# Sigmoid attention and MLP on one core: one wait ahead of each attention group, and a fourth of the attention's rate during the half-size up products

## The chip, the core and the metric

The kernel runs on one core of a Trainium2 chip. The metric is the device time of one execution in microseconds (us): median of 3 runs, 1158.67 us before the change (1157.67 to 1159.39). A profile of one execution goes with it. Engines are named as in the profile: PE is the matrix engine (TensorE), PEld its weight loads, DVE VectorE, ACT ScalarE, POOL GpSimd, SP the engine that issues most DMAs.

## The reference

Sigmoid attention over 8 batches, 12 heads, 448 positions and head size 64, in float32, followed by a two-layer MLP with a piecewise quadratic between the layers (768 to 2048 to 768 wide, 3584 tokens):

```python
scores = scale * np.matmul(q, k.transpose(0, 1, 3, 2)) - np.log(S)
attn = 1.0 / (1.0 + np.exp(-scores))
x = np.matmul(attn, v)            # then (B, H, S, D) -> (B*S, H*D)
h = x @ w_in
g = np.where(h >= 1, h, np.where(h <= -1, 0.0, (h + 1) ** 2 / 4))
out = g @ w_out
```

## The kernel before

**Attention.** Two heads make a pair; a batch has 6 pairs, the whole run 48. The 448 keys of a pair are cut into 4 pieces: c = 0, 1 and 2 with 128 keys each, and the "mid" piece c = 3 with the last 64 keys of both heads stacked. `load_pair` fetches q, k and v, `prep_a` finds maxima (on ACT), `prep_b` splits each float32 operand into two float16 halves (on POOL from pair 17 on) and sends them by DMA into the layout `qk`. `scores` makes the products of queries and keys into a PSUM tile `psc` (two buffers, so piece i reuses the buffer of piece i - 2), `weigh` applies the sigmoid in place (ACT, L450), and splits the result into a high half (ACT, L458) and a low half (DVE, L459) in `ahl`. `av` multiplies these with v into `pav`. From pair 14 on (`NFULL + NHALF`) `step` works on two pieces at once: `scores` of a group of two pieces, then `av` of the group before it. At a pair's last piece `av` ends with a copy into `x32` (ACT, L500) and a maximum `xm` (DVE, L501).

PE works on three kinds of product here. Full-array products take all 128 rows and columns: up (`ph`, L685 and L719), down (`po`, L755), the first part of the scores (L409 with `qk`, L404 for the mid piece), the column sums and maxima with `one` (L155, L171). The score corrections L418 take 64 rows, and the products with v L491 put out 64 columns; two of these that follow each other with different halves run side by side.

**MLP.** The attention of batch b + 1 is done while the MLP of batch b runs. For batch 2 and later (`SB`) the up projection is done in half-size products: 16 blocks of hidden units are treated as 8 pairs, each with 7 units of 9 matmuls over 224 columns (`up_blocks`), 56 units in all. They are followed by 48 down units (`downs`), each of 6 matmuls over 448 columns, 288 in all. `bend`, the activation between the layers, works on ACT and DVE during the up units.

**The order.** The loop at the end of the function (L894 to L930) emits units one by one, and between them steps of the attention, at a rate given by `share`: each of the first 92 units (`last`) counts `DW` = 8 in batches 2 to 7, so 56/92 of a batch's 24 pieces are emitted during the up units and the rest during the first 36 down units. At unit 92 `start_blocks` and `finish_blocks` are emitted: they take the maximum over the batch's x (`xm1`, L523), put it on a diagonal (`diag`, L161), spread it with a matmul (L171), reduce it (L172), make scales of it (L127 to L135), and split sums and differences of x (L534 to L537, on DVE and POOL) into the operands of the next batch's up products (L540 on ACT, L541 on DVE, seven of each). Which instruction stands where on each engine is settled at build time, by a scheduler that takes what is emitted first by preference but passes over what it holds not to be ready. On the chip each engine then goes through its instructions in that fixed order.

Of the kernel before, what the change touches and what calls it, by code (L numbers as in the profile page):

```python
# [14 lines left out]
F32 = mybir.dt.float32  # L15
# [8 lines left out]
P = 128  # L24
# [29 lines left out]
QA = 17  # L54
QT = 3
CORN = 10
TP = 1

DW = 8
MIX0 = 24  # L60
MIX1 = 96
Q_PRIO = 72
# [7 lines left out]
def sigmoid_attention_mlp(ctx: ExitStack, tc: tile.TileContext, first_qvk, qkv, w_in, w_out, out_t):  # L70
# [312 lines left out]

    pieces = {}

    def scores(todo):

        tiles = []
        for i in todo:
            p, c = divmod(i, NPC)  # L390
            mid = c == NKC
            w = slice(c * P, S if mid else (c + 1) * P)
            psc = ps_sc.tile([P, 2, 512], F32, tag="psc", name="psc")
            tiles.append(psc)
            if p < NFULL:
                r = ready[p][0]
                for j in range(2):
                    out = psc[j * D : (j + 1) * D, 0, :S] if mid else psc[:, j, :S]
                    rows = slice(j * D, (j + 1) * D)
                    nc.tensor.matmul(out, r[rows, 2, w], r[rows, 0, :], start=True, stop=True)  # L400
            elif mid and p >= NFULL + NHALF:
                hl = ready[p][4]
                for t, (kh, qh) in enumerate(((0, 0), (1, 0), (0, 1))):
                    nc.tensor.matmul(psc[:, 0, :S], corner(p)[:, kh, :], hl[:, 0, qh, :], start=t == 0, stop=t == 2)  # L404
            else:
                kq = ready[p][0]
                for j in range(2):
                    out = psc[j * D : (j + 1) * D, 0, :S] if mid else psc[:, j, :S]
                    nc.tensor.matmul(out, kq[:, j, 1, w], kq[:, j, 0, :], start=True, stop=False)  # L409
        for i, psc in zip(todo, tiles):  # L410
            p, c = divmod(i, NPC)
            mid = c == NKC
            if p >= NFULL and not (mid and p >= NFULL + NHALF):
                hl, w = ready[p][4], slice(c * P, S if mid else (c + 1) * P)
                for j in range(2):
                    rows = slice(j * D, (j + 1) * D)
                    out = psc[rows, 0, :S] if mid else psc[:, j, :S]
                    nc.tensor.matmul(out, hl[rows, 1, 0, w], hl[rows, 0, 1, :], start=False, stop=True)  # L418
            if mid and p >= NFULL + NHALF and p + 2 in maxes:

                sums[p + 2] = all_sum(maxes[p + 2], 3, psc[:, 1, :])
        for i, psc in zip(todo, tiles):
            weigh(i, psc)
        for p, c in (divmod(i, NPC) for i in todo):
# [13 lines left out]
    def weigh(i, psc):  # L438
# [5 lines left out]
        sqk = 1.0 / math.sqrt(D) if p < NFULL else ready[p][2][:, 0:1]  # L444
        if p < NFULL + NHALF:
            a32 = att_p.tile([P, 2, S], F32, tag="ahl", name="a32")
            nc.scalar.activation(a32[:, :n, :], a, AF.Sigmoid, bias=nls, scale=sqk)  # L447
            pieces[i] = a32
            return
        nc.scalar.activation(a, a, AF.Sigmoid, bias=nls, scale=sqk)  # L450
# [5 lines left out]
            parts = [(a, ahl[:, 0], ahl[:, 1])]  # L456
        for x, hi, lo in parts:
            nc.scalar.activation(hi, x, AF.Copy, scale=ATT)  # L458
            nc.vector.scalar_tensor_tensor(out=lo, in0=x, scalar=ATT, in1=hi, op0=ALU.mult, op1=ALU.subtract)  # L459
        pieces[i] = ahl  # L460

    state = {"scored": 0}

    def av(i):
        p, c = divmod(i, NPC)
        b, hp = divmod(p, NP)
        if c == 0:
            state["pav"] = ps_av.tile([P, 512], F32, tag="pav", name="pav")
            if hp == 0:
                state["xm"] = sml_p.tile([P, NP], F32, tag="xm", name="xm", bufs=2)  # L470
        pav = state["pav"]
        at = pieces.pop(i)
        mid = c == NKC
        v = ready[p][1]
        split = p >= NFULL + NHALF
        terms = []
        for j in range(2):
            o = slice(j * D, (j + 1) * D)
            full_v = slice((2 * c + j) * D, (2 * c + j + 1) * D)
            if p < NFULL and mid:  # L480
                full_v = slice(2 * c * D, (2 * c + 1) * D)
            if not split:
                r = o if mid else slice(0, P)
                terms.append([(v[r, full_v], at[r, 0 if mid else j, :])])
            elif mid:
                terms.append([(v[:, vh, full_v], at[:, 0, j, :]) for vh in range(2)])
            else:
                terms.append([(v[:, vh, full_v], at[:, ah, j, :]) for vh, ah in ((0, 0), (1, 0), (0, 1))])
        for t in range(len(terms[0])):
            for j in range(2):  # L490
                nc.tensor.matmul(  # L491
                    pav[j * D : (j + 1) * D, :S], *terms[j][t],
                    start=c == 0 and t == 0, stop=mid and t == len(terms[j]) - 1,
                )
# [296 lines left out]
    def step(i):  # L791
# [6 lines left out]
        if c == 2:  # L798
            prep_b(p + 2)
            if late:  # L800
                prep_a(p + 3)
        if i < NPC * (NFULL + NHALF):
            more, some = i + LAG + 1, [i]
        else:

# [4 lines left out]
        if more > state["scored"]:  # L810
            scores(range(state["scored"], more))
            state["scored"] = more
        for k in some:
            av(k)


    wi = Weight(w_in, w_in_sb, "wi", [5 + 2 * (f % 6) for f in range(NFC)])
# [76 lines left out]
    for b in range(1, B):  # L894
# [75 lines left out]
```

## Time and profile before

| what | value |
|---|---|
| median of 3 runs | 1158.67 us |
| the profiled execution | 1159.12 us |
| its span, from the first to the last instruction | 1157.4 us |
| busy DVE / ACT / POOL | 815.8 / 722.1 / 294.4 us |
| mean granted clock of PE | 0.999 |
| matmuls recorded | 7662 |

The span is the time that the instructions of the core take; 1.7 us lie around it. The busy time of PE in the profile is made of modelled ends of pipelined matmuls, so two matmuls that follow each other overlap in it; how fast PE really goes is read from the starts of successive rows.

### The profile page before, as it was taken

What the parts mean: (1) busy time and instruction counts of PE and PEld (TensorE: products, weight loads), DVE (VectorE), ACT (ScalarE), POOL (GpSimd) and SP (SyncE); (2) the same over time, 40 slices, a digit from 0 to 9 for tenths busy, and PEclk for the clock granted to TensorE, in tenths of its full rate; (3) what the DMA queues carried; (4) which work ended last, traced back from release to release, by engine and by line L of the source; (5) the groups of instructions that cost most, each with busy time, mean ns of one, the idle gap of its engine ahead of it and who ended that gap; (6) DMA issues with size and microseconds to landing.
All of it is one profiled execution on the core that took longest, in us unless ns stands there. A gap on an engine that the chain in (4) does not pass through costs nothing.

```text
span 1157.4 us, 20215 instructions
## 1 busy us (share of the span) xinstructions
PE 1135.0 (98%) x7662; PEld 666.1 (58%) x7662; DVE 815.8 (70%) x1730; ACT 722.1 (62%) x1199; POOL 294.4 (25%) x367
## 2 busy tenths in 40 slices
PE   8899999999999999999999999999999999999998
PEld 2234334444446775567745785457854677558954
DVE  6988886879987895468936787367964589646820
ACT  6978888578666784557754786447764576423410
POOL 0000000001542354324523353325344233210000
PEclk9999999999999999999999999999999999999999
DMA  9943443162564654225632465224742165203300
GB/s 366 380 138 135 143 165 97 50 212 105 192 209 144 239 211 127 76 94 205 219 102 65 145 207 203 66 66 147 264 145 76 53 207 200 100 17 123 133 22 27
DMA packets 58112, 170.00 MB, mean 147 GB/s; under 512 B 8608, under 2 KB 39840, under 8 KB 51872
## 3 DMA queue, kind: packets, MB, share of 16 engines
q1 hardware_dynamic: 56288, 159.29, 39.9%
q10 hardware_dynamic: 1728, 9.44, 2.3%
q8 instruction: 60, 0.98, 0.3%
q14 instruction: 36, 0.29, 0.1%
HBM read 126.94 MB, written 23.40 MB: 130 GB/s over the span
## 4 chain that ended last, share of the span: by engine, by line
PE 76%; DMA 8%; DVE 6%; ACT 4%; POOL 3%; issue 1%; SPq 0%; POOLq 0%; DVEq 0%; ACTq 0%
PE po L755 30%; PE ph L685 23%; PE pav L491 8%; PE ph L719 7%; DMA raw<-qkv 4%; PE psc L409 3%; PE psc L418 3%; DMA w_out_sb<-w_in 2%; PE psc L404 1%; DVE ahl L459 1%; ACT psc L450 1%; POOL hl L373 1%; DVE mixa L625 1%; ACT dump L335 1%; POOL raw L371 1%
## 5 line engine op out<-in xcount | busy, mean ns | idle before, releaser
L755 PE MATMUL po<-ghl,w_out_sb 128*128 128x448 f16 x2304 | 446.9, 353 | 1.8 <-ACT ghl L735 1.8
L755 PEld LDWEIGHTS <-w_out_sb 128*128 128x128 f16 x2304 | 221.5, 98 | 217.2 <-issue 17.6
L685 PE MATMUL ph<-w_in_sb 128*128 128x224 f16 x3024 | 307.7, 259 | 1.7 <-DMA w_in_sb<-blocks 1.3
L685 PEld LDWEIGHTS <-w_in_sb 128*128 128x128 f16 x3024 | 282.6, 98 | 31.1 <-issue 27.6
L459 DVE SCALAR_TENSOR_TENSOR ahl<-psc,ahl 128x896 f16<-128x896 f32 (+1 forms) x170 | 153.0, 900 | 98.8 <-ACT ahl L458 96.9
L450 ACT ACTIVATE psc<-psc,nls,sqk 128x896 f32<-128x896 f32 (+1 forms) x136 | 129.8, 971 | 94.0 <-PE psc L418 76.1
L371 POOL TENSOR_SCALAR raw<-raw,qkv_s 128x448 f32<-128x448 f32 (+1 forms) x93 | 70.9, 777 | 443.8 <-DVE qkv_i L135 355.7
L458 ACT ACTIVATE ahl<-psc 128x896 f16<-128x896 f32 (+1 forms) x170 | 127.0, 762 | 30.6 <-DVE ahl L459 29.4
L719 PE MATMUL ph<-xhl,w_in_sb 128*128 128x448 f16 x576 | 112.5, 353 | 0.0
L335 ACT ACTIVATE dump<-raw 128x448 f16<-128x448 f32 (+1 forms) x105 | 61.6, 587 | 72.0 <-DMA raw<-qkv 71.3
L694 DVE TENSOR_TENSOR xhl<-ph,xhl 128x224 f32<-128x224 f32 x240 | 87.7, 383 | 26.0 <-PE ph L685 19.6
L491 PE MATMUL pav<-ahl,v 128*64 128x448 f16 x748 | 98.2, 360 | 0.4 <-DVE ahl L459 0.4
L735 ACT ACTIVATE ghl<-g 128x448 f16<-128x448 f32 x128 | 72.5, 572 | 37.2 <-DVE g L734 36.7
L732 ACT ACTIVATE g<-xhl,hr,ihr 128x448 f32<-128x448 f32 x96 | 68.7, 752 | 41.8 <-DVE xhl L694 40.8
L736 DVE TENSOR_TENSOR ghl<-g,ghl 128x448 f16<-128x448 f32 x128 | 84.2, 664 | 8.2 <-ACT ghl L735 7.7
L733 DVE SCALAR_TENSOR_TENSOR g<-g,rk 128x448 f32<-128x448 f32 x112 | 79.8, 727 | 13.9 <-ACT g L732 13.5
L719 PEld LDWEIGHTS <-w_in_sb 128*128 128x128 f16 x576 | 54.8, 98 | 58.2 <-issue 8.9
L373 POOL TENSOR_TENSOR hl<-raw,hl 128x448 f16<-128x448 f32 x62 | 72.8, 1194 | 0.0
L409 PE MATMUL psc<-qk 128*128 128x448 f16 x252 | 66.4, 354 | 2.8 <-ACT a L447 1.8
L734 DVE SCALAR_TENSOR_TENSOR g<-xhl,ihs,g 128x448 f32<-128x448 f32 x96 | 66.3, 708 | 0.3
L768 DVE TENSOR_SCALAR o<-po,od 128x448 f32<-128x448 f32 x42 | 28.5, 679 | 53.1 <-PE po L755 53.1
L430 POOL COPY w_in_sb<-hl 64x128 f16<-64x128 f16 x68 | 32.4, 476 | 127.3 <-DVE hl L367 125.4
(151 smaller groups left out, 1131.6 us busy)
## 6 DMA issues: line engine op xcount, KB each, us to landing
w_in_sb<-blocks SPq DMA_DIRECT2D x48, 1344.0 KB, 6.6
raw<-qkv SPq DMA_DIRECT2D x34, 704.0 KB, 4.8
qk<-hl SPq DMA_DIRECT2D x320, 56.0 KB, 2.0
w_out_sb<-w_in SPq DMA_DIRECT2D x16, 768.0 KB, 11.1
out_t<-o SPq DMA_DIRECT2D x48, 224.0 KB, 1.9
blocks<-mixs SPq DMA_DIRECT2D x8, 768.0 KB, 3.5
w_out_sb<-w_out ACTq DMA_DIRECT2D x6, 768.0 KB, 4.6
raww<-w_out ACTq DMA_DIRECT2D x6, 768.0 KB, 5.8
```

The lines of the kernel that those rows point to most:

```text
L371: nc.gpsimd.tensor_scalar(out=rt, in0=rt, scalar1=s[:, t : t + 1], scalar2=1.0, op0=ALU.mult, op1=ALU.mult)
L373: nc.gpsimd.tensor_tensor(out=dst[:, 1, :], in0=rt, in1=hi, op=ALU.subtract)
L409: nc.tensor.matmul(out, kq[:, j, 1, w], kq[:, j, 0, :], start=True, stop=False)
L450: nc.scalar.activation(a, a, AF.Sigmoid, bias=nls, scale=sqk)
L458: nc.scalar.activation(hi, x, AF.Copy, scale=ATT)
L459: nc.vector.scalar_tensor_tensor(out=lo, in0=x, scalar=ATT, in1=hi, op0=ALU.mult, op1=ALU.subtract)
L491: nc.tensor.matmul(pav[j * D : (j + 1) * D, :S], *terms[j][t], start=c == 0 and t == 0, stop=mid and t == len(terms[j]) - 1,)
L685: nc.tensor.matmul(out, w[:, wt, wh, c * P : (c + 1) * P], xc[:, xt, c, xh, :], start=j in (0, 2) and c + wh + xh == 0, stop=c == HC - 1 a ...
L694: add = lambda out, q, other: nc.vector.tensor_tensor(out=out, in0=quarter(q), in1=other, op=ALU.add)
L719: nc.tensor.matmul(ph[:, :S], w_in_sb[:, f, wh, c * P : (c + 1) * P], xhl[:, c, xh, :], start=c == 0 and wh + xh == 0, stop=c == NCC - 1 a ...
L736: (nc.gpsimd if f % GPOOL else nc.vector).tensor_tensor(out=ghl[:, f, 1, :], in0=g, in1=hi, op=ALU.subtract)
L755: nc.tensor.matmul(po[:, :S], w_out_sb[:, f, wh, m * P : (m + 1) * P], ghl[:, f, gh, :], start=f == lo and wh + gh == 0, stop=f == hi - 1 ...
```

## The change

It has three parts. First, `when_made` collects the instructions that end the making of the group's inputs, from pair 14 on (`GROUPED`), and `once` makes the first matmul of the group wait for all of them: for `scores` the pieces whose `psc` buffers it takes over, for `av` the pieces that it multiplies. `av` now takes the whole group. Second, in `scores` the order of the two heads' first products is turned round, and the column sums (`all_sum`) are emitted ahead of the score corrections instead of behind them. Third, from batch 2 on each of the 56 half-size up units counts `UW` = 2 in `share` and each down unit 8 as before. So 112 of 400 shares, 28% of the 24 pieces, are emitted during the up units, where it was 61%, and 72% during the 36 down units, where it was 39%. What is computed is the same: 7486 matmuls are issued by both.

```diff
+GROUPED = 14
...
-DW = 8
+DW, UW = 8, 2
...
+    made = {}
+
+    def when_made(some):
+
+        waits = [ins for i in some if i >= NPC * GROUPED for ins in made.get(i, ())]
+
+        def once(ins):
+            while waits:
+                tc.add_manual_dep(
+                    ins.ins, waits.pop().ins.name,
+                    mybir.DependencyInfo(mybir.DependencyClass.Sync, mybir.DependencyReason.DATA), reason="group",
+                )
+
+        return once
+
     def scores(todo):
 
+        once = when_made(i - 2 for i in todo)
...
-                    nc.tensor.matmul(out, r[rows, 2, w], r[rows, 0, :], start=True, stop=True)
+                    once(nc.tensor.matmul(out, r[rows, 2, w], r[rows, 0, :], start=True, stop=True))
...
-                for j in range(2):
+                for j in (1, 0):
                     out = psc[j * D : (j + 1) * D, 0, :S] if mid else psc[:, j, :S]
-                    nc.tensor.matmul(out, kq[:, j, 1, w], kq[:, j, 0, :], start=True, stop=False)
+                    once(nc.tensor.matmul(out, kq[:, j, 1, w], kq[:, j, 0, :], start=True, stop=False))
+        for i, psc in zip(todo, tiles):
+            p, c = divmod(i, NPC)
+            if c == NKC and p >= NFULL + NHALF and p + 2 in maxes:
+
+                sums[p + 2] = all_sum(maxes[p + 2], 3, psc[:, 1, :])
...
-            if mid and p >= NFULL + NHALF and p + 2 in maxes:
-
-                sums[p + 2] = all_sum(maxes[p + 2], 3, psc[:, 1, :])
...
-            nc.vector.scalar_tensor_tensor(out=lo, in0=x, scalar=ATT, in1=hi, op0=ALU.mult, op1=ALU.subtract)
+            made.setdefault(i, []).append(nc.vector.scalar_tensor_tensor(
+                out=lo, in0=x, scalar=ATT, in1=hi, op0=ALU.mult, op1=ALU.subtract
+            ))
...
-    def av(i):
+    def av(some):
+
+        once = when_made(some)
+        for i in some:
...
-        if i < NPC * (NFULL + NHALF):
+        if i < NPC * GROUPED:
             more, some = i + LAG + 1, [i]
...
-        for k in some:
-            av(k)
+        av(some)
...
-        share = [DW // 2 if b < SB and u < NA * NCC // 2 else DW for u in range(last)]
+        mixed_up = 7 * NFC // 2 if b >= SB else 0
+        share = [UW if u < mixed_up else DW // 2 if b < SB and u < NA * NCC // 2 else DW for u in range(last)]
```

How the change moves instructions is seen at three places. (Line numbers of the changed kernel are higher: L426 is the old L409, L440 the old L418, L515 the old L491, L709 the old L685, L779 the old L755, L172 the old L171.)

The first place is PE during the up units of a batch. Before, a pair of score corrections (`psc<-hl`) stood apart in the order, with 18 up matmuls (`ph`) between them:

```order
L409 MATMUL psc<-qk 128x448
L418 LDWEIGHTS hl
L418 MATMUL psc<-hl 128x448
L685 LDWEIGHTS w_in_sb
L685 MATMUL ph<-w_in_sb 128x224
...
L418 LDWEIGHTS hl
L418 MATMUL psc<-hl 128x448
L685 LDWEIGHTS w_in_sb
```

After, in most groups the four corrections of a group stand together, with the products with v (`pav`) right behind them:

```order
L440 LDWEIGHTS hl
L440 MATMUL psc<-hl 128x448
L440 LDWEIGHTS hl
L440 MATMUL psc<-hl 128x448
L515 LDWEIGHTS v
L515 MATMUL pav<-ahl,v 64x448
```

Over the whole program, the places on PE where a matmul follows one of another kind (full array, 64 rows, 64 columns) go from 506 to 410, and the stretches of the 64-row or 64-column kind with an odd number of matmuls, in which one has no partner, from 68 to 26.

The second place is PE where batch 6 ends and batch 7 begins. Before, the maximum of batch 7's x (`psc<-diag`) stood among the down matmuls of batch 6, 54 of them behind the last product with v and 66 ahead of the first up matmul of batch 7:

```order
L755 LDWEIGHTS w_out_sb
L755 MATMUL po<-ghl,w_out_sb 128x448
L171 LDWEIGHTS one
L171 MATMUL psc<-diag,one 128x128
L755 LDWEIGHTS w_out_sb
L755 MATMUL po<-ghl,w_out_sb 128x448
```

After, it stands right between the last product with v and the first up matmul, and no down matmul is left there:

```order
L515 LDWEIGHTS v
L515 MATMUL pav<-ahl,v 64x448
L172 LDWEIGHTS one
L172 MATMUL psc<-diag,one 128x128
L709 LDWEIGHTS w_in_sb
L709 MATMUL ph<-w_in_sb 128x224
```

At the ends of batches 2 to 5 it is alike, with attention of the batch after next in between. All 288 down matmuls stand ahead of the last group's 10 products with v. From there to the first up matmul come, at the ends of batches 2, 3 and 5: one piece's scores (4 matmuls), the diagonal, another piece's scores (4), 12 products with v, the mid piece's 3 score products and a column sum. At the end of batch 4 they are: one piece's scores, the diagonal, the scores of c = 2 and mid (2 + 3 + 2 and the sum), 12 products with v. In front of the last 10 products with v stand one piece's scores, and before these 26 down matmuls (11 at the end of batch 4; 35, with no scores between, at the end of batch 6). At the end of batch 1, 42 down matmuls stay ahead of the diagonal and 28 behind it. In the down stretches of batches 2 to 6 there are now some seven groups, with 38 to 54 down matmuls between them, where there were four with 42 to 54.

The third place is DVE where batch 2 ends. Before, one low half of the next attention (`ahl`) stood between the batch's last maximum (`xm`) and the reduction of the diagonal product (`xm_5021<-psc`), ahead of the `diag` row:

```order
L501 TENSOR_REDUCE xm<-x_92 128x1
L536 TENSOR_TENSOR xhl<-x_92,xhl 128x672
L459 SCALAR_TENSOR_TENSOR ahl<-psc,ahl 128x896
L523 TENSOR_REDUCE xm_5021<-xm 128x1
L768 TENSOR_SCALAR o<-po,od 128x448
L161 TENSOR_SCALAR diag<-ident,xm_5021 128x128
L172 TENSOR_REDUCE xm_5021<-psc 128x1
```

After, there are two, one on each side of `diag`:

```order
L525 TENSOR_REDUCE xm<-x_92 128x1
L560 TENSOR_TENSOR xhl<-x_92,xhl 128x672
L547 TENSOR_REDUCE xm_5021<-xm 128x1
L478 SCALAR_TENSOR_TENSOR ahl<-psc,ahl 128x896
L162 TENSOR_SCALAR diag<-ident,xm_5021 128x128
L478 SCALAR_TENSOR_TENSOR ahl<-psc,ahl 128x896
L173 TENSOR_REDUCE xm_5021<-psc 128x1
```

More of the change, by code (lines that the diff above doesn't have):

```diff
@@ L403, in scores @@
                 for t, (kh, qh) in enumerate(((0, 0), (1, 0), (0, 1))):
-                    nc.tensor.matmul(psc[:, 0, :S], corner(p)[:, kh, :], hl[:, 0, qh, :], start=t == 0, stop=t == 2)
+                    once(nc.tensor.matmul(psc[:, 0, :S], corner(p)[:, kh, :], hl[:, 0, qh, :], start=t == 0, stop=t == 2))
             else:
                 kq = ready[p][0]
-                for j in range(2):
+                for j in (1, 0):
                     out = psc[j * D : (j + 1) * D, 0, :S] if mid else psc[:, j, :S]
-                    nc.tensor.matmul(out, kq[:, j, 1, w], kq[:, j, 0, :], start=True, stop=False)
+                    once(nc.tensor.matmul(out, kq[:, j, 1, w], kq[:, j, 0, :], start=True, stop=False))
[3 more added lines that the diff above has]
+                sums[p + 2] = all_sum(maxes[p + 2], 3, psc[:, 1, :])
         for i, psc in zip(todo, tiles):
@@ L446, in weigh @@
             a32 = att_p.tile([P, 2, S], F32, tag="ahl", name="a32")
-            nc.scalar.activation(a32[:, :n, :], a, AF.Sigmoid, bias=nls, scale=sqk)
+            made[i] = [nc.scalar.activation(a32[:, :n, :], a, AF.Sigmoid, bias=nls, scale=sqk)]
             pieces[i] = a32
@@ L458, in weigh @@
             nc.scalar.activation(hi, x, AF.Copy, scale=ATT)
-            nc.vector.scalar_tensor_tensor(out=lo, in0=x, scalar=ATT, in1=hi, op0=ALU.mult, op1=ALU.subtract)
+            made.setdefault(i, []).append(nc.vector.scalar_tensor_tensor(
+                out=lo, in0=x, scalar=ATT, in1=hi, op0=ALU.mult, op1=ALU.subtract
+            ))
         pieces[i] = ahl
     state = {"scored": 0}
-    def av(i):
[L465 to L489, printed above, removed]
-            for j in range(2):
[L491 to L494, printed above, removed]
@@ new lines, in av @@
+    def av(some):
+        once = when_made(some)
+        for i in some:
+            p, c = divmod(i, NPC)
+            b, hp = divmod(p, NP)
+            if c == 0:
+                state["pav"] = ps_av.tile([P, 512], F32, tag="pav", name="pav")
+                if hp == 0:
+                    state["xm"] = sml_p.tile([P, NP], F32, tag="xm", name="xm", bufs=2)
+            pav = state["pav"]
+            at = pieces.pop(i)
+            mid = c == NKC
+            v = ready[p][1]
+            split = p >= NFULL + NHALF
+            terms = []
+            for j in range(2):
+                o = slice(j * D, (j + 1) * D)
+                full_v = slice((2 * c + j) * D, (2 * c + j + 1) * D)
+                if p < NFULL and mid:
+                    full_v = slice(2 * c * D, (2 * c + 1) * D)
+                if not split:
+                    r = o if mid else slice(0, P)
+                    terms.append([(v[r, full_v], at[r, 0 if mid else j, :])])
+                elif mid:
+                    terms.append([(v[:, vh, full_v], at[:, 0, j, :]) for vh in range(2)])
+                else:
+                    terms.append([(v[:, vh, full_v], at[:, ah, j, :]) for vh, ah in ((0, 0), (1, 0), (0, 1))])
+            for t in range(len(terms[0])):
+                for j in range(2):
+                    once(nc.tensor.matmul(
+                        pav[j * D : (j + 1) * D, :S], *terms[j][t],
+                        start=c == 0 and t == 0, stop=mid and t == len(terms[j]) - 1,
+                    ))
```

## The prediction, made before the changed kernel ran

> **What bounds the kernel now.** I read the page first: the busy shares and the chain that ended last.
>
> ```profile
> span 1157.4 us, 20215 instructions
> PE 1135.0 (98%) x7662; PEld 666.1 (58%) x7662; DVE 815.8 (70%) x1730; ACT 722.1 (62%) x1199; POOL 294.4 (25%) x367
> PE 76%; DMA 8%; DVE 6%; ACT 4%; POOL 3%; issue 1%; SPq 0%; POOLq 0%; DVEq 0%; ACTq 0%
> ```
>
> PE is busy for 98% of the span. The next view is a window over batches 2 to 7, where most of the change lies; after the bounds come its length and PE's busy time.
>
> ```profile
> 400.00:1150.00 750.00, 745.73 (x5519) 486.77 (x5518) 489.23 (x1082) 417.29 (x720) 238.37 (x296) 1.00 0.38 130
> ```
>
> Only 750.0 - 745.7 = 4.3 us of idle PE are left there. So waits can give back at most about 4 us; what else there is to gain lies in how matmuls follow each other. For that the third view is PE's timeline around a group (start, time, instruction, count).
>
> ```profile
> 1013.65 0.54 PE L409 MATMUL psc<-qk 128*128 128x448 f16 x2
> 1014.03 0.73 PE L404 MATMUL psc<-hl,w_in_sb 128*128 128x448 f16 x3
> 1014.69 0.36 PE L418 MATMUL psc<-hl 64*128 64x448 f16 x2
> 1014.98 1.33 PE L491 MATMUL pav<-ahl,v 128*64 128x448 f16 x12
> 1016.24 9.25 PE L755 MATMUL po<-ghl,w_out_sb 128*128 128x448 f16 x48
> 1025.43 1.14 PE L491 MATMUL pav<-ahl,v 128*64 128x448 f16 x10
> 1026.50 10.39 PE L755 MATMUL po<-ghl,w_out_sb 128*128 128x448 f16 x54
> ```
>
> Read the starts, not the times: a full-array matmul of 448 columns takes (1014.03 - 1013.65)/2 = 0.19 us. The three L404 take 0.66 us up to L418, 0.09 to 0.10 more than three times 0.19: that is what a change of kind costs. The pair of L418 takes 0.29, one slot of 0.19 and again 0.10. A pair costs one slot, since its halves run side by side. So each group pays 0.096 us three times or more.
>
> **The change, part by part.** *Fewer changes of kind.* In PE's order the changes of kind go from 506 to 410, so 96 x 0.096 = 9.2 us go. A half without a partner takes a slot of its own, as here among the up products of before:
>
> ```profile
> 955.58 0.36 PE L418 MATMUL psc<-hl 64*128 64x448 f16 x1
> 955.88 1.90 PE L685 MATMUL ph<-w_in_sb 128*128 128x224 f16 x18
> 957.71 0.36 PE L418 MATMUL psc<-hl 64*128 64x448 f16 x1
> 958.00 1.04 PE L685 MATMUL ph<-w_in_sb 128*128 128x224 f16 x9
> ```
>
> Each single L418 holds PE for 0.29 us, as long as the pair above. Stretches with an odd half go from 68 to 26: two of them make one pair's extra slot, so 21 slots x 0.19 = 4.0 us go. Together **13.2 us**, on the path because PE is it.
>
> *The waits of a group's first product* add no instruction, and PE's queue behind one holds whatever follows in the fixed order, a down or up product. What covers it: in the new order at least 38 down products (38 x 0.19 = 7.2 us) and 10 or 12 products with v (1.1 us) lie between a group's scores and the next group's first product. What they cover is the chain from scores to low halves, as it ran in the profile:
>
> ```profile
> 1014.80 1.69 ACT L450 ACTIVATE psc<-psc,nls,sqk 128x448 f32<-128x448 f32 x2 [5.91 <-PE psc L404]
> 1016.52 1.34 ACT L458 ACTIVATE ahl<-psc 128x896 f16<-128x896 f32 x2
> 1017.47 1.74 DVE L459 SCALAR_TENSOR_TENSOR ahl<-psc,ahl 128x896 f16<-128x896 f32 x2 [6.68 <-ACT ahl L458]
> 1019.24 0.54 ACT L458 ACTIVATE ahl<-psc 64x448 f16<-64x448 f32 x1 [1.39 <-DVE ahl L459]
> 1019.81 0.63 DVE L459 SCALAR_TENSOR_TENSOR ahl<-psc,ahl 64x448 f16<-64x448 f32 x1 [0.60 <-ACT ahl L458]
> ```
>
> From the end of L418 (1014.69 + 0.36 = 1015.05) to the last low half (1020.44) are 5.4 us, under 8.3. I cost the waits at nothing, with 4.2 us either way as bounds: the idle PE time of the window, gone or once more.
>
> *The rate.* Attention comes later in a batch, and its last group now stands behind all down products. At the batch's end lies the one chain that nothing else on PE can cover: from the last products with v over the maximum of x to the first up product. The profile shows it at the end of batch 6:
>
> ```profile
> 1026.61 0.64 ACT L500 ACTIVATE x<-pav,sqk 128x448 f32<-128x448 f32 x1 [6.83 <-PE pav L491]
> 1027.27 0.62 DVE L501 TENSOR_REDUCE xm<-x 128x1 f32<-128x448 f32 x1 [5.59 <-ACT x L500]
> 1027.81 1.89 DVE L536 TENSOR_TENSOR xhl<-x,xhl 128x672 f32<-128x672 f32 x1
> 1029.62 0.15 DVE L523 TENSOR_REDUCE xm<-xm 128x1 f32<-128x6 f32 x1
> 1029.78 1.60 POOL L537 TENSOR_TENSOR xhl<-x,xhl 128x672 f32<-128x672 f32 x1 [0.80 <-DVE xm L523]
> 1029.80 1.62 DVE L161 TENSOR_SCALAR diag<-ident,xm 128x128 bf16<-128x128 bf16 x1
> 1036.72 0.22 PE L171 MATMUL psc<-diag,one 128*128 128x128 bf16 x1
> 1037.87 0.86 ACT L540 ACTIVATE w_in_sb<-x,x_s 128x672 f16<-128x672 f32 x1 [10.62 <-DVE x_s L131]
> 1038.76 0.92 DVE L541 SCALAR_TENSOR_TENSOR w_in_sb<-x,x_s,w_in_sb 128x672 f16<-128x672 f32 x1
> ```
>
> The products with v end at 1025.43 + 1.14 = 1026.57, `diag` at 1031.42: 4.85 us. From the diagonal's product (1036.72) to the first operand's low half (1039.68) are 2.96 us. In all 7.8 us, covered before by 54 and 66 down products. In the new order they are gone, and the second up product needs that low half.
>
> - End of batch 6: nothing lies between. **7.8 us** of waiting.
> - Ends of batches 2, 3 and 5: two low halves of the next attention (1.09 us each, row below) stand in DVE's chain, +2.2. The first lets POOL finish before `diag`, which then takes 0.24 instead of 1.62, -1.4. Chain 8.6 us. PE's work between, by the starts above: two pieces' scores 2 x (0.38 + 0.29), 12 products with v 1.26, mid scores 0.66: 3.3 us. Left **5.3 us**, three times, 15.9.
> - End of batch 4: only one low half in the chain, 7.8 + 1.1 = 8.9, less 3.4 of work: 5.5. Ahead of it 11 down products (2.1) and 12 with v (1.3) cover 3.4 of the 5.4 us chain above: 2.0 more. **7.5 us**.
> - End of batch 1: 42 and 28 down products stay (8.0 and 5.3 us): nothing.
>
> Sum 31.2 us. What bounds it are the spread of two steps and a slower case of the same chain (min/median/max in ns in the first two rows; the end of batch 4 in the others):
>
> ```profile
> L536 DVE TENSOR_TENSOR xhl<-x,xhl x6: 1142/1287/1889, 339.7 to 1027.8; 128x672 f32<-128x672 f32 x6
> L161 DVE TENSOR_SCALAR diag<-ident,xm x8: 237/460/1624, 62.3 to 1029.8; 128x128 bf16<-128x128 bf16 x8
> 750.66 1.14 PE L491 MATMUL pav<-ahl,v 128*64 128x448 f16 x10
> 753.62 1.09 DVE L459 SCALAR_TENSOR_TENSOR ahl<-psc,ahl 128x896 f16<-128x896 f32 x1 [4.08 <-ACT ahl L458]
> 758.39 0.65 DVE L161 TENSOR_SCALAR diag<-ident,xm 128x128 bf16<-128x128 bf16 x1
> ```
>
> With both steps at their shortest a chain is 0.75 + 1.38 = 2.1 us shorter: 31.2 - 5 x 2.1 = 20.7. At the end of batch 4 it took 759.04 - 751.80 = 7.2 us to `diag`, 2.4 more than 4.85: with that in the four middle ends, 40.8. I take 31.2, whose rows have the same steps in the same order. [...]
>
> *PE's clock.* The new waits ahead of the diagonal are 3.9 us at the middle ends (4.85 + 1.09 - 1.38 - 0.67 of scores) and 4.9 us at the last. What such a gap does to the clock is seen from both sides (the two PE rows are of the cold start):
>
> ```profile
> PE psc L171 <- DVE diag L161: 2.1, 1, 2.1
> 1150.00:1157.40 7.40, 3.71 (x20) 1.72 (x18) 0.69 (x1) 0.00 (x0) 0.00 (x0) 0.91 0.08 31
> 4.44 4.85 PE L400 MATMUL psc<-ghl 64*128 64x448 f32 x12 [4.44 <-DMA ghl<-first_qvk]
> 10.12 0.97 PE L400 MATMUL psc<-ghl 64*64 64x448 f32 x4
> ```
>
> A wait of 2.1 us left the clock alone, while in the 3.7 us after the last matmul it fell (mean 0.91). Twelve first matmuls took 4.8 us; at the later pace of four in 0.9 they take 2.7. So a gap costs between 0 and 2.1 us, 0 to 10.4 for five. The gaps are a little longer than 3.7, but the work behind the diagonal waits another 1.4 us for its chain anyway (5.3 - 3.9), which hides part of a slow clock; I take half: **5 us**. [...]
>
> **Sum**, against the profiled execution's 1159.1 us (0.45 above the median of the runs): 1159.1 - 13.2 + 31.2 + 5 = **1182 us**.
>
> **The rivals.** *Faster:* the ends of the batches are nearly covered. It decides at 13.2/5 = 2.6 us lost per end. With the shortest steps and no low half waiting in between, a middle chain takes 0.64 + 0.62 + 1.14 + 0.15 + 0.24, some 2.9 us with handing over, up to the diagonal; less 0.67 of scores, 2.2 are lost, and the 2.7 of work behind it covers the rest. Five ends then cost 4 x 2.2 + 4.9 = 13.7, and with the 4.2 us of idle time gone the kernel takes 1159.1 - 13.2 + 13.7 - 4.2 = 1155 us. Against it: DVE's new order puts the low halves of the next attention into the chain. Chance 0.09.
>
> *The rate does not take:* the scheduler could have put the groups where they were; then only the 13.2 us count, 1146 us. PE's order shows seven groups instead of four in the down products. Chance 0.01.
>
> *The down stretches starve:* seven groups in the place of four ask more of ACT, which stands in order behind raw loads:
>
> ```profile
> ACT dump L335 <- DMA raw<-qkv: 71.3, 14, 8.5
> ```
>
> The slack of a group is 8.3 - 5.4 = 2.9 us. If one wait of this mean (71.3/14 = 5.1 us) hit each of three pairs in five batches, 15 x 2.2 = 33 us would come on top: 1215 us. For it: pairs follow each other faster; against it: before, these waits reached PE hardly at all. Chance 0.06.
>
> *The clock* stays up (1177) or falls five times at the full price (1187). Of the forecast's chance below, 0.20 goes to the first and 0.30 to the second, since the new gaps are longer than the 3.7 us in which it fell. [...]
>
> **How the numbers follow.** Forecast with its bounds for chain and clock 0.75; partly covered ends, 1162 to 1168, 0.06; between the two signs 0.03; the rivals 0.09, 0.01 and 0.06. Lowest by the bounds: 1159.1 - 13.2 - 4.2 + 20.7 = 1162; highest 1159.1 - 13.2 + 4.2 + 40.8 + 10.4 = 1201, of which I cut the last 4, since all bounds would have to meet. Range 1162 to 1197. A measurement of this kernel tells 0.2% (2.3 us) from no change: faster 0.10, same 0.03, slower 0.87.
>
> **What would show it.** Right: in PE's waits, ones of 3 to 5 us for `diag` and 1 to 3 us for the first up product's operands, at five batch ends; the granted clock under 1.00 right behind some of them; down and up stretches shorter, with hardly a single L418 (L440). Wrong: if PE at these ends waits under 2.6 us in all, the chain was sized wrongly; if it waits for low halves within the down stretches, the cover was; if the stretches between ends are not some 13 us shorter in sum, a change of kind or an odd half costs less than read here.

## The result and the profile after

The changed kernel takes **1213.72 us** (median of 4 runs, 1211.34 to 1217.06); the kernel before, on the same chip, 1158.19 us. The ratio is 1.048, 95% interval 1.0452 to 1.0508: 4.8% slower. The prediction was 1182 us in a range of 1162 to 1197: the sign was right, the size half of what came. The profiled execution took 1211.34 us, 52.2 us more than that of before, and its span is longer by the same 52.2 us. One execution of `r2_av` below (1194.54 us, at a granted clock of 0.948) was in a slower state of the chip, and the ratio given there leaves it out. First the page of after (the span, the busy time of the engines, the chain's shares by engine):

```profile
span 1209.6 us, 20250 instructions
PE 1139.3 (94%) x7662; PEld 671.6 (56%) x7662; DVE 835.3 (69%) x1730; ACT 725.1 (60%) x1199; POOL 294.3 (24%) x367
PE 61%; DVE 14%; ACT 9%; DMA 6%; issue 5%; POOL 3%; SPq 1%; POOLq 0%; DVEq 0%; ACTq 0%
```

PE's share of the chain went from 76% to 61%; DVE's and ACT's, 10% together before, are 23%. The engines do hardly more work (DVE 835.3 us for 815.8); PE waits for them. The same window as before (its length, busy time of PE, PEld, DVE, ACT and POOL, then the granted clock) and PE's waits:

```profile
400.00:1150.00 750.00, 702.01 (x5263) 464.09 (x5261) 502.56 (x1076) 424.62 (x728) 246.16 (x307) 0.97 0.39 128
```

```profile
PE psc L172 <- DVE diag L162: 20.5, 5, 4.9
PE psc L426 <- DVE ahl L478: 14.1, 9, 5.0
PE ph L709 <- DVE xhl L718: 10.0, 9, 2.9
PE ph L709 <- DMA w_in_sb<-blocks: 2.1, 1, 2.1
PE ph L709 <- ACT w_in_sb L564: 1.8, 1, 1.8
```

Idle PE in the window is 750.0 - 702.0 = 48.0 us where it was 4.3. There are five waits for `diag`, one at each of five batch ends. But there are also 10 us in which up products wait for `xhl` (L718, the additions that take an up product out of its PSUM quarter `ph`), which no step of the prediction has. The longest of these, 2.90 us, is not the doing of a group: near the end of batch 6's up units a reduction (L340) stands ahead of L718 in DVE's order and waits for a raw load.

```profile
1011.53 1.68 DVE L340 TENSOR_REDUCE m<-raw 128x2 f32<-128x896 f32 x2 [4.31 <-DMA raw<-qkv]
1013.13 0.38 DVE L718 TENSOR_TENSOR xhl<-ph,xhl 128x224 f32<-128x224 f32 x1
1013.56 0.64 PE L709 MATMUL ph<-w_in_sb 128*128 128x224 f16 x5 [2.90 <-DVE xhl L718]
```

And the mean clock, 1.00 in this window before, is 0.97.

**A batch's end**, on the timeline at the end of batch 5 (start, time, engine, instruction; in brackets the idle time ahead and what ended it):

```profile
942.82 1.14 PE L515 MATMUL pav<-ahl,v 128*64 128x448 f16 x10
943.88 0.55 PE L426 MATMUL psc<-qk 128*128 128x448 f16 x2
944.37 0.36 PE L440 MATMUL psc<-hl 64*128 64x448 f16 x2
945.23 1.29 DVE L560 TENSOR_TENSOR xhl<-x,xhl 128x672 f32<-128x672 f32 x1
946.51 1.08 DVE L478 SCALAR_TENSOR_TENSOR ahl<-psc,ahl 128x896 f16<-128x896 f32 x1
947.51 1.51 DVE L162 TENSOR_SCALAR diag<-ident,xm 128x128 bf16<-128x128 bf16 x1
949.08 0.29 PE L172 MATMUL psc<-diag,one 128*128 128x128 bf16 x1 [4.34 <-DVE diag L162]
951.42 2.41 PE L515 MATMUL pav<-ahl,v 128*64 128x448 f16 x12
954.37 1.89 PE L709 MATMUL ph<-w_in_sb 128*128 128x224 f16 x18
```

PE stands for 4.34 us; the low half of the next attention is in the chain, as reckoned. `diag` takes 1.51 us, while a difference of x runs beside it on POOL:

```profile
947.38 1.59 POOL L559 TENSOR_TENSOR xhl<-x 128x672 f32<-128x672 f32 x1
```

Then look at L515: 12 products with v take 2.4 us, where 10 took 1.14. That is the clock. The same stretch and the one behind it as windows:

```profile
946.80:953.60 6.80, 3.81 (x17) 1.24 (x17) 6.58 (x18) 3.36 (x5) 6.74 (x7) 0.50 0.36 85
953.70:960.50 6.80, 6.07 (x61) 5.57 (x60) 6.80 (x24) 5.87 (x10) 0.76 (x1) 1.00 0.18 73
```

The clock is at 0.50 for the whole first window, that is until 4.5 us after PE had work again.

**Up units behind a batch's end**, in after:

```profile
512.87 0.90 DVE L565 SCALAR_TENSOR_TENSOR w_in_sb<-x,x_s,w_in_sb 128x672 f16<-128x672 f32 x1
513.82 0.90 DVE L565 SCALAR_TENSOR_TENSOR w_in_sb<-xhl,x_s,w_in_sb 128x672 f16<-128x672 f32 x1
515.80 0.38 DVE L718 TENSOR_TENSOR xhl<-ph,xhl 128x224 f32<-128x224 f32 x1
516.10 1.07 DVE L478 SCALAR_TENSOR_TENSOR ahl<-psc,ahl 128x896 f16<-128x896 f32 x1
516.23 1.02 PE L709 MATMUL ph<-w_in_sb 128*128 128x224 f16 x9 [0.55 <-DVE xhl L718]
517.32 0.62 DVE L478 SCALAR_TENSOR_TENSOR ahl<-psc,ahl 64x448 f16<-64x448 f32 x1
517.97 0.99 DVE L718 TENSOR_TENSOR xhl<-ph,xhl 128x224 f32<-128x224 f32 x3
518.71 1.50 PE L709 MATMUL ph<-w_in_sb 128*128 128x224 f16 x14 [1.46 <-DVE xhl L718]
```

DVE first has the last splits of x (L565) to do, which lay beside down products before, and then the low halves of an attention group (L478); the additions L718, for which PE waits 0.55 and 1.46 us, stand behind both.

**Where the 52.2 us are.** I took all starts of matmuls in a trace, and for each step from one start to the next the median step between the same two kinds in the trace of before (where it has no such step, the kind's slot and 0.096 us for a change). The sum of these is the column "order". What a step is longer goes to "idle" if it is over 0.15 us and PE was out of work, to "clock" if it lies in a half-clock stretch, and otherwise to "rest". In us against the same count of before:

| kernel | order | idle | clock | rest | span |
|---|---|---|---|---|---|
| after | -12.8 | +52.3 | +15.7 | -3.2 | +52.2 |
| rate 8, waits kept (rate8) | -18.1 | +22.0 | +5.2 | -2.6 | +6.5 |
| rate 6, waits kept (rate6) | -13.4 | +17.6 | +6.3 | -3.1 | +7.2 |
| rate 2, no waits (rate2_nowait) | +12.2 | -2.6 | +2.5 | +1.7 | +14.2 |
| rate 2, wait ahead of the scores only (r2_sc) | +10.3 | +26.1 | +8.8 | +0.4 | +45.4 |
| rate 2, wait ahead of `pav` only (r2_av) | +1.9 | +11.9 | +3.9 | -0.9 | +16.9 |
| rate 8, wait ahead of `pav` only (r8_av) | -9.4 | +9.5 | +1.7 | -1.0 | +0.8 |
| the same from pair 18 on (r8_av18) | -7.8 | +3.3 | +2.5 | -1.4 | -3.5 |
| rate 8, no waits (nowait8) | -3.1 | +2.9 | +2.0 | -2.2 | -0.4 |

After's new idle time falls in three parts: 32.7 us at the batch ends (26.1 ahead of the diagonal, 6.6 between it and the first up product), 15.7 in the first 30 us of the up units (2.1 of it the wait for `w_in_sb<-blocks`, of which before had one of 1.3), and some 4 in the attention of pairs 14 to 17 and elsewhere, the 2.90 behind a raw load among them.

### The profile page after: what moved, and what is told of

It is laid out like the page before. It is cut to its first block, busy times and chain, and to the rows that moved or that the text cites. A ratio compares the mean times of both kernels' runs of the same rounds, so it can differ in the third digit from the quotient of the medians.

```text
span 1209.6 us, 20250 instructions
## 1 busy us (share of the span) xinstructions
PE 1139.3 (94%) x7662; PEld 671.6 (56%) x7662; DVE 835.3 (69%) x1730; ACT 725.1 (60%) x1199; POOL 294.3 (24%) x367
## 4 chain that ended last, share of the span: by engine, by line
PE 61%; DVE 14%; ACT 9%; DMA 6%; issue 5%; POOL 3%; SPq 1%; POOLq 0%; DVEq 0%; ACTq 0%
PE po L779 27%; PE ph L709 13%; PE ph L743 8%; PE pav L515 6%; DVE ahl L478 3%; DMA raw<-qkv 3%; PE psc L426 3%; DVE w_in_sb L565 3%; DMA w_in_sb<-blocks 2%; PE psc L440 2%; ACT psc L469 2%; ACT dump L336 1%; ACT ahl L477 1%; DVE xhl L718 1%; POOL raw L372 1%
## 5 line engine op out<-in xcount | busy, mean ns | idle before, releaser
L779 PE MATMUL po<-ghl,w_out_sb 128*128 128x448 f16 x2304 | 447.0, 353 | 0.5 <-ACT w_out_sb L278 0.5
L779 PEld LDWEIGHTS <-w_out_sb 128*128 128x128 f16 x2304 | 221.3, 98 | 218.6 <-issue 17.8
L709 PE MATMUL ph<-w_in_sb 128*128 128x224 f16 x3024 | 303.6, 260 | 16.3 <-DVE xhl L718 10.0
L709 PEld LDWEIGHTS <-w_in_sb 128*128 128x128 f16 x3024 | 287.4, 98 | 34.0 <-issue 28.3
L478 DVE SCALAR_TENSOR_TENSOR ahl<-psc,ahl 128x896 f16<-128x896 f32 (+1 forms) x170 | 152.6, 899 | 130.3 <-ACT ahl L477 128.3
L718 DVE TENSOR_TENSOR xhl<-ph,xhl 128x224 f32<-128x224 f32 x240 | 85.7, 383 | 27.7 <-PE ph L709 25.5
L515 PE MATMUL pav<-ahl,v 128*64 128x448 f16 x748 | 95.9, 379 | 0.0
L336 ACT ACTIVATE dump<-raw 128x448 f16<-128x448 f32 (+1 forms) x105 | 61.8, 589 | 56.8 <-DMA raw<-qkv 55.5
L757 DVE SCALAR_TENSOR_TENSOR g<-g,rk 128x448 f32<-128x448 f32 x112 | 85.6, 777 | 11.3 <-ACT g L756 11.1
L743 PEld LDWEIGHTS <-w_in_sb 128*128 128x128 f16 x576 | 55.1, 98 | 59.6 <-issue 9.7
L760 DVE TENSOR_TENSOR ghl<-g,ghl 128x448 f16<-128x448 f32 x128 | 81.4, 648 | 9.6 <-ACT ghl L759 8.9
L426 PE MATMUL psc<-qk 128*128 128x448 f16 x252 | 66.8, 365 | 17.5 <-DVE ahl L478 14.1
L758 DVE SCALAR_TENSOR_TENSOR g<-xhl,ihs,g 128x448 f32<-128x448 f32 x96 | 75.8, 811 | 0.1
L449 POOL COPY w_in_sb<-hl 64x128 f16<-64x128 f16 x68 | 37.0, 544 | 134.4 <-DVE hl L368 132.5
```

The lines of the kernel that those rows point to most:

```text
L426: once(nc.tensor.matmul(out, kq[:, j, 1, w], kq[:, j, 0, :], start=True, stop=False))
L478: made.setdefault(i, []).append(nc.vector.scalar_tensor_tensor(out=lo, in0=x, scalar=ATT, in1=hi, op0=ALU.mult, op1=ALU.subtract))
L515: once(nc.tensor.matmul(pav[j * D : (j + 1) * D, :S], *terms[j][t], start=c == 0 and t == 0, stop=mid and t == len(terms[j]) - 1,))
L709: nc.tensor.matmul(out, w[:, wt, wh, c * P : (c + 1) * P], xc[:, xt, c, xh, :], start=j in (0, 2) and c + wh + xh == 0, stop=c == HC - 1 a ...
L718: add = lambda out, q, other: nc.vector.tensor_tensor(out=out, in0=quarter(q), in1=other, op=ALU.add)
L743: nc.tensor.matmul(ph[:, :S], w_in_sb[:, f, wh, c * P : (c + 1) * P], xhl[:, c, xh, :], start=c == 0 and wh + xh == 0, stop=c == NCC - 1 a ...
```

## The experiments

Theory A is the prediction's: a group's waits are free, and the loss lies in bare batch ends and the clock. By its rivals the waits cost time in themselves: in the up units (E), in the down units (F), or through the one ahead of the scores (G). Ratios are to the kernel before, with their 95% intervals.

**The old rate with the waits** (`rate8`).

```diff
-DW, UW = 8, 2
+DW, UW = 8, 8
```

> The waits of the changed kernel, the rate of before (UW = 8). Theory A (the loss lies at the batch ends, where the rate pushed the last group behind all down products): the ends are covered again (48 down products ahead of the diagonal, 52 behind it), and only the better order of matmuls is left: 369 changes of kind for 506 (137 x 0.096 = 13.2 us) and 12 odd stretches for 68 (28 slots x 0.19 = 5.3 us), so 1158.2 - 18.5 = 1140 us. Rival B (the group's wait itself holds PE, as the 14.1 us of PE waits for low halves in the changed kernel suggest): 1158 - 18 + 14 = 1154 us or more.

Measured: 1166.72 us, ratio 1.007 (1.0047 to 1.0093). A's 1140 is missed by 27 us; B had said 1154 or more. The order got 18.1 us cheaper, and the new idle time took 22.0 of it back. Windows over the attention of pairs 14 to 23 (first row; 14 to 17 are done by some 360 us) and over four whole batches:

```profile
230.00:502.00 272.00, 259.60 (x1706) 149.56 (x1705) 204.12 (x395) 180.21 (x297) 89.94 (x107) 0.99 0.48 163
502.00:1060.00 558.00, 544.68 (x4145) 362.66 (x4143) 381.54 (x867) 340.73 (x577) 196.67 (x250) 1.00 0.40 134
```

The same windows before:

```profile
230.00:502.00 272.00, 269.06 (x1749) 150.94 (x1748) 209.48 (x419) 185.82 (x305) 90.26 (x107) 1.00 0.48 164
502.00:1060.00 558.00, 555.26 (x4164) 362.35 (x4162) 381.22 (x845) 335.42 (x574) 200.83 (x250) 1.00 0.40 135
```

PE's idle time went from 2.9 to 12.4 us in the first and from 2.7 to 13.3 in the second. The batch ends are covered here, so this is what the waits cost here by themselves. (The longest single wait, 3.92 us for L718 at 375 us, has a raw load in its chain as well: ACT had stood 4.36 us for one ahead of the group's sigmoid.) One place of the second window, in the up units:

```profile
537.62 1.05 ACT L469 ACTIVATE psc<-psc,nls,sqk 128x896 f32<-128x896 f32 x1
539.82 1.05 ACT L469 ACTIVATE psc<-psc,nls,sqk 128x896 f32<-128x896 f32 x1
542.26 1.09 DVE L478 SCALAR_TENSOR_TENSOR ahl<-psc,ahl 128x896 f16<-128x896 f32 x1 [0.18 <-ACT ahl L477]
543.80 0.68 DVE L718 TENSOR_TENSOR xhl<-ph,xhl 128x224 f32<-128x224 f32 x2
544.53 1.69 PE L709 MATMUL ph<-w_in_sb 128*128 128x224 f16 x16 [1.66 <-DVE xhl L718]
```

The two pieces of a group reach ACT and then DVE one right behind the other, and L718 stands behind the low half in DVE's order. PE does not wait at the group; it stops some 5 us after the group's first sigmoid began (544.53 - 1.66 = 542.87), at an up product without a free `ph` quarter.

**The new rate without waits** (`rate2_nowait`): in after, `waits = []`; the edits of the program's order stay.

> The rate of the changed kernel (UW = 2), without the waits. In its order the batch ends are covered (41 down products ahead of the diagonal, 43 behind), but there are 611 changes of kind (105 more than before, 10.1 us) and 92 odd stretches (24 more, 12 slots, 2.3 us). Theory A (the rate hurts only through the ends, and only together with the waits): 1158.2 + 12.4 = 1171 us, no wait of PE for the diagonal, clock 1.00. Rival C (the rate itself starves attention or the up products, whatever the waits): some 1171 + 16 to 1171 + 50 us, with PE waiting for DVE in the up and down stretches.

Measured: 1171.16 us, 1.0107 (1.0086 to 1.0128), as A said. Hardly a wait is left (window from 360 to 1150 us):

```profile
360.00:1150.00 790.00, 787.45 (x5815) 507.56 (x5814) 533.53 (x1147) 450.65 (x775) 244.37 (x318) 1.00 0.40 130
```

In its order 41 down products stand ahead of the diagonal and 43 behind it at the ends of batches 2 to 5. So the rate alone does not bare the ends. It costs through its order, with 611 changes of kind instead of 506.

**A rate between** (`rate6`): rate8 with `UW = 6`.

> The waits, and a rate between (UW = 6). Ends covered (48 ahead of the diagonal, 35 behind), 405 changes of kind (101 fewer, 9.7 us), 24 odd stretches (22 slots, 4.2 us). Theory A: 1158.2 - 13.9 = 1144 us. Rival C (the loss grows with the rate): a third of the way from 1140 to 1214, some 1160 us.

Measured: 1166.35 us, 1.0062 (1.0038 to 1.0086). The ends have 48 and 35 down products, and 17.6 us of new idle time still stand against 13.4 gained by the order. A falls for the waits a second time, and C's 1160 is missed by 6 us: the loss does not grow with the rate step by step.

**Keeping the clock up** (`warm`): in after, PE gets 16 products whose result nobody uses ahead of each diagonal. (Only extra work; nothing is left out.)

```diff
+        pav, n = state["pav"], 512 - S
+        for _ in range(WARM):
+            nc.tensor.matmul(
+                pav[:, S:], x32[:, NP - 1, :P], x32[:, NP - 1, :n], start=True, stop=True, skip_group_check=True
+            )
```

> The changed kernel, with 16 small float32 matmuls on x ahead of each diagonal product, whose results nobody reads: PE has work in the gap and its clock should stay up. Theory A with the clock as a cost of its own: the 11 to 12 us that matmuls lose in half-clock stretches go, so 1213.7 - 11.5 = 1202 us, granted clock 0.99 or more. Rival D (a slow clock falls together with waiting that is there anyway and costs nothing): 1213 us, within 2.

Measured: 1208.59 us, 1.0428 (1.0409 to 1.0446), between the two. Behind 300 us the half-clock time fell from 44.4 to 20.5 us (the sums of the clock's stretches in the traces; the mean clock of the profiled execution went from 0.980 to 0.990), and the median by 5.1: 0.21 us per us of half clock, or more, if the extra products cost something themselves. At the end of batch 5 a wait of 5.3 us remained ahead of them, so the cure is partial. Nor is it the extra work alone that differs: ahead of the last group's products with v and one piece's scores there are now 11 down products in place of 26 at the ends of batches 3 and 5, and 26 in place of 11 at that of batch 4.

**Waits in the up units only, or in the down units only, at the old rate** (`r8_up`, `r8_down`; both keep them while the attention of pairs 14 to 17 runs, up to about 360 us).

```diff
+                state["wait"] = b < SB or u < mixed_up
...
-        waits = [ins for i in some if i >= NPC * GROUPED for ins in made.get(i, ())]
+        waits = [ins for i in some if state["wait"] and i >= NPC * GROUPED for ins in made.get(i, ())]
```

(For `r8_down` the first line has `u >= mixed_up`.)

> Rate of before; the waits only for groups emitted during batch 1 and during the up units of later batches. 422 changes of kind for 506 (8.1 us), 32 odd stretches for 68 (18 slots, 3.4 us), ends covered. Theory E (in the up units a group that is held together lands as one burst on ACT and DVE, and the up products wait behind it for their PSUM tiles): the run with the waits everywhere missed its 1140 us by 27 us; most of it comes from these waits, so 1158 - 11.5 + 16 to 20 = 1163 to 1167 us, with PE waits for xhl (L718) of 8 us or more. Rival F (the waits cost in the down units): 1147 us.

> Rate of before; the waits only for groups emitted during batch 1 and during the down units of later batches. 463 changes of kind (4.1 us), 52 odd stretches (8 slots, 1.5 us), ends covered. Theory E: no burst in the up units, 1158 - 5.6 + 0 to 4 (batch 1) = 1152 to 1157 us, PE waits for xhl at most 4 us. Rival F: 1158 - 6 + 16 = 1168 us or more.

Measured: 1168.51 us, 1.0079 (1.0055 to 1.0102), and 1168.7 us, 1.0081 (1.0056 to 1.0107). By the medians neither E nor F is right for both: r8_up lies 1.5 us above E's range, r8_down meets F's number. The windows tell them apart, r8_up first:

```profile
230.00:502.00 272.00, 259.76 (x1693) 148.11 (x1691) 206.58 (x401) 182.93 (x301) 89.32 (x107) 0.98 0.48 162
502.00:1060.00 558.00, 548.33 (x4113) 358.72 (x4112) 378.52 (x857) 335.39 (x572) 196.64 (x250) 1.00 0.40 134
```

and r8_down, with one row of its timeline:

```profile
230.00:502.00 272.00, 259.71 (x1691) 147.41 (x1689) 209.02 (x400) 184.16 (x302) 91.46 (x107) 0.99 0.48 162
502.00:1060.00 558.00, 554.80 (x4144) 360.05 (x4143) 382.33 (x857) 335.66 (x572) 199.40 (x250) 1.00 0.40 135
```

```profile
333.57 0.55 PE L426 MATMUL psc<-qk 128*128 128x448 f16 x2 [3.02 <-DVE ahl L478]
```

In the four whole batches r8_down has 3.2 us of idle PE, next to the 2.7 of before, and r8_up 9.7: in the down units the waits are covered, as the prediction said; in the up units they are not. What hides this in the medians is the first window, with 12.2 and 12.3 us. Up to 360 us both lose the same, 6.3 and 6.2 us where before lost 2.7: there the waits of pairs 14 to 17 stand, one of them 3.02 us long. From there to 502 us the two lose the same for different reasons. r8_up loses 6.0 us, 4.13 of it in one wait for L718 among batch 2's up products, again with a raw load in its chain. r8_down loses 6.1, 3.19 of it in one wait for the operands `w_in_sb<-blocks` from DMA at 412 us. No wait of an up product for L718 is on record in r8_down.

**No wait ahead of the scores, at the old rate** (`r8_av`).

```diff
-        once = when_made(i - 2 for i in todo)
+        once = when_made(())
```

> Rate of before; the wait only ahead of a group's products with v, not ahead of its scores. 434 changes of kind (6.9 us), 42 odd stretches (13 slots, 2.5 us), ends covered. Theory G (it is the wait ahead of the scores, for both PSUM buffers at once, that makes the burst): 1158 - 9.4 = 1149 us, hardly any PE wait for xhl. If holding a group together is enough, whichever wait does it: 1160 to 1166 us.

Measured: 1159.53 us, 1.0002 (0.9989 to 1.0015): by the time G is refuted at its full size, since 1149 was not reached. But 0.7% against rate8 is gone, some 8 us, and the waits of up products for L718 fall from 12.7 to 1.3 us. The wait ahead of the scores makes the burst. The one ahead of `pav` still leaves 9.5 us of new idle time, most of it again ahead of 502 us (9.1 us idle in that window, where before had 2.9).

**Waits in the down units only, at the new rate** (`r2_down`): after with the edit of r8_down.

> The changed rate (UW = 2); the waits only for groups emitted during batch 1 and during the down units. 438 changes of kind (6.5 us), 36 odd stretches (16 slots, 3.0 us); the ends of batches 2 to 6 are bare as in the changed kernel. Theory A + clock: the ends cost what they cost there, 33 us of waiting and 11 us of slow clock, while the first up products behind them wait again for DVE (16 us) because of what the end leaves queued there: 1158 - 9.5 + 33 + 11 + 16 = 1209 us. Theory E for the up units: those 16 us come from the grouped waits and go, 1193 us.

Measured: 1198.11 us, 1.0332 (1.0307 to 1.0357), between the two expectations. The waits of up products for L718 fall from 10.0 to 4.3 us. Right behind the bare ends, where after has most of them, there are none left: at the end of batch 2 the first 63 up products (from 508.20 us) run without a break, although DVE has the same splits to do.

```profile
508.20 7.66 PE L709 MATMUL ph<-w_in_sb 128*128 128x224 f16 x63
```

So the bare end alone does not make them wait there, as A had it; it takes the groups held together, as E said. The 4.3 us that remain (none over 0.9) lie 26 and 49 us behind the first up product, and what makes them is open. The ends of batches 2 to 5 stay bare, with 22 products with v right ahead of the diagonal.

**Which wait bares the ends** (`r2_sc`: after without the wait ahead of `pav`; `r2_av`: after without the one ahead of the scores).

> The rate of 2 with the wait ahead of the scores alone (none ahead of pav). Theory S: it is this wait, together with the rate, that leaves the batch ends without down products and drops the clock. The order alone then costs +10.2 us against before (1168), the bare ends some 32 and the clock 12 to 15, the up units up to 16: 1205 to 1225. Rival: the ends need both waits: then the order and the known waits alone, 1168 to 1185. In the profile theory S wants waits of PE for diag of 4 to 5 us at the ends of batches 2 to 5 and half-clock stretches behind them.

> The rate of 2 with the wait ahead of pav alone (none ahead of the scores). Theory S: the batch ends keep their down products, the clock stays up, and the order costs +1.8 us against before: 1160, with 3 to 9 us of waits for attention pieces 1163 to 1169. Rival: any group wait at this rate bares the ends: 1195 to 1215. In the profile theory S wants no wait for diag over 1 us at the ends of batches 2 to 5 and a mean clock of 0.99 or more.

Measured: 1204.23 us, 1.0386 (1.0365 to 1.0406), and 1175.74 us, 1.0138 (1.0116 to 1.016). The end of batch 5 in r2_sc:

```profile
944.21 0.57 PE L515 MATMUL pav<-ahl,v 128*64 128x448 f16 x4
945.57 0.76 PE L515 MATMUL pav<-ahl,v 128*64 128x448 f16 x6 [0.79 <-DVE ahl L478]
946.39 0.22 PE L172 MATMUL psc<-diag,one 128*128 128x128 bf16 x1
949.09 0.26 PE L709 MATMUL ph<-w_in_sb 128*128 128x224 f16 x1
```

No down product stands between the last products with v and the first up product, while r2_av has 38 or 41 ahead of it and 18 or 28 behind it at the ends of batches 2 to 5. So it is the rate together with the wait ahead of the scores that bares the ends, and the rival of r2_sc falls. Why the scheduler builds it so is open. The waits of r2_sc are shorter than I expected: the mean clock is 0.991, against 0.980 in after, and the time lies 1 us below the range that I gave. r2_av lies 7 us above its range: 11.9 us of new idle time instead of 3 to 9, and 3.9 of clock, whose two half-clock stretches lie ahead of 300 us, where the rate is that of before; the second follows this wait:

```profile
286.19 5.25 PE L743 MATMUL ph<-xhl,w_in_sb 128*128 128x448 f16 x18 [2.13 <-DVE g L758]
```

By this, a part of what r2_av loses beyond its range belongs to the attention of pairs 14 to 17, where only the waits and the order edits are new. What makes the rest of the 7 us is open.

**The edits of the program's order alone** (`nowait8`: `waits = []` and `UW = 8`) **and the best of the pieces** (`r8_av18`: r8_av with `NPC * 18` for `NPC * GROUPED`).

> The old rate of 8 and no group wait at all: only the program-order edits are left (groups from pair 14, second high half first, the sum of the maxima behind the group's scores). Counted with the row times of before, its order is 3.2 us cheaper: 1155 if these edits do nothing else; 1159 or more if they make waits of their own, as the higher times of the kernels with waits would allow.

> The old rate of 8 and the wait ahead of pav alone, from pair 18 on, so that the pairs 14 to 17 go without. Its order is 7.9 us cheaper than that of before: 1150 with no new wait. If the 9.5 us of new waits of the kernel with the same wait from pair 14 were those of batch 1 for the most part, 1151 to 1155; if they lie in each batch, 1157 to 1160.

Measured: 1161.03 us, 1.0011 (0.9998 to 1.0024), and 1156.51 us, 0.9983 (0.9968 to 0.9999). The order edits alone change nothing that can be told from noise, although their order is 3.1 us cheaper by the count; the expected "1159 or more" came. r8_av18 lies between the two ranges that were given, half a microsecond below the second. Without the waits of pairs 14 to 17, r8_av gains another 0.2% and is the only kernel here below the one before, by 0.17%, which is at the edge of what can be measured. Its windows:

```profile
230.00:502.00 272.00, 267.63 (x1750) 151.16 (x1747) 212.30 (x422) 185.06 (x304) 91.29 (x107) 1.00 0.48 164
502.00:1060.00 558.00, 552.11 (x4202) 366.80 (x4199) 389.30 (x851) 336.71 (x578) 201.23 (x250) 1.00 0.40 136
```

In the first window the idle time falls from 9.1 to 4.4 us, as expected; in the second it is 5.9, twice that of before, in exchange for the cheaper order.

## Why the prediction was half the size

- **Fewer changes of kind and fewer odd halves: right.** -13.2 us were reckoned, the count of the trace gives -12.8. The price of 0.096 us for a change, read from three starts, is also the median over the whole trace of before (0.285 us from one kind to another, 0.189 within a kind). What passes inside the array at a change, the trace does not show.
- **The bare batch ends: right in sum, in part by luck.** 31.2 us were reckoned and 32.7 measured. Ahead of the diagonal the middle ends lost 4.42 us (3.9 reckoned) and the last 4.98 (4.9); the end of batch 4, where a further wait stood ahead of the scores, 7.84 (5.9). That the middle ends came within 0.5 us is in part two errors that cancel: `diag` took 1.51 us there instead of 0.24, beside POOL's L559, which I had taken to be over by then, and L560 took 1.29 instead of 1.89. Behind the diagonal 0.94 us were lost at most ends instead of 1.4, and at another place: at the next scores, which waited for a low half. The first up product waited for its operands (1.83 us) at the end of batch 6 alone. The lower bound of 20.7 was also wrong in itself: at three ends it takes off 1.38 us for a short `diag` that the 31.2 already has short. Without that it is 31.2 - 5 x 0.75 - 2 x 1.38 = 24.7, and the range would begin at 1166.
- **"I cost the waits at nothing, with 4.2 us either way": this is the step that failed.** The cover was worked out for PE's queue in the down units, and there it holds (r8_down: 3.2 us idle against 2.7). The step asked only what PE does while the group is being made. It did not ask what a group made as a whole does on ACT and DVE, where in the up units the additions that free `ph` stand behind it. Instead of nothing, some 20 us were lost: some 16 at the start of the up units, and some 4 elsewhere, of which one wait of 3.0 us stands in the attention of pairs 14 to 17. Not all of it is the groups' doing, since the 2.90 us behind a raw load and a part of the 2.1 us for `w_in_sb<-blocks` are in it. r8_up (waits in the up units) shows the mechanism with the ends covered, r8_av (no wait ahead of the scores) takes most of it away, and in r2_down (no waits in the up units) the waits behind the bare ends are gone.
- **The clock: mechanism right, size wrong.** 5 us were taken from a range of 0 to 10.4. Measured are 15.7, of which 2.5 lie in a stretch of 3.41 us at 59 us (before has none there, but PE's order is the same in both kernels up to 78 us, so it cannot be put down to the change), 1.7 behind a wait of 3.0 us that ends at 334.5 us, and 11.5 at the batch ends: six stretches, 1.9 us each, near the 2.1 that was the upper bound for one gap. That nearness proves little: the 2.1 came from the first twelve matmuls (4.44 to 9.29 us), and the profile shows no half clock there: its records of the clock begin at 9.19 us, at 1.00. My reason for half of it, that the work behind the diagonal waits for its chain anyway, did not hold: at most ends the waits behind the diagonal fell by 0.5 us (1.4 less 0.94), not by half of 2.1. The end of batch 4 also had two stretches instead of one, as its chain has two waits.
- **The rivals.** "The down stretches starve" gave 1215, nearly the measured time, but the 33 us that it added were not lost by its mechanism. The raw loads ended 71.3 us of ACT's idle time before and 55.5 now, r8_down lost 0.5 us more than before in its four whole batches, and in after one wait of 2.90 us is on record that goes back to a raw load, over DVE and in the up units. That the number fits is chance. The clock fell at every end, at a little over the rival's full price (11.5 us for 10.4). "The rate does not take" and the covered ends did not.

```profile
ACT dump L336 <- DMA raw<-qkv: 55.5, 14, 7.0
```

The error was 29 us of 52 (52.2 measured, 23.0 reckoned): about 20 by waits that were costed at nothing and 11 by the clock, less small terms.

## What to carry to other kernels

A wait that holds several pieces together does not end where it is waited for: what it releases arrives in one lump at the engines behind, so look there for work that frees a buffer, and price its delay, before the wait is called free. A rate that moves work from one half of a loop to the other should be judged by what stands around the chain at the loop's end in the built order; here the rate alone left the chain covered, and so did the waits alone; together they took every down product away from it. And a gap on PE can be paid twice: the batch ends of after cost 32.7 us in waiting and 11.5 in clock.

## What the runs showed of the hardware

The clock fell in steps that I had not expected: of the eight half-clock stretches in after two lasted 3.41 us and six, all at the batch ends, 6.83 us. Gaps of 4.3 to 5 us at the batch ends gave 6.83, although at the end of batch 5 PE was at work again for the last 4.5 us of it, and so did a gap of 2.58 us ahead of the diagonal at the end of batch 4. The length of a gap alone does not decide. The wait of 3.02 us shown for r8_down stands at that place in after, rate8, rate6, r8_up and `warm` too; in `warm` the 12 products with v behind it took 1.33 us, in the other five 1.80 to 2.45, since there the clock fell behind the wait (0.51 in after from 336.0 to 339.3 us). The wait of 2.1 us for `diag` before left the clock up. The one of 2.13 us in r2_av did not: of the 18 products behind it, in 5.25 us, those from 287.9 to 290.5 us ran at 0.37 us each, twice the 0.19 of full clock. What else decides is open.

Of the 47.8 us at half clock in after 15.7 were lost, a third, as PE waits for other engines in part of such a stretch anyway: in the window shown at the end of batch 5 it was busy for 3.81 of the 6.80 us.
